# A new hand-listed order of the same steps for chunked attention and a gated convolution

## The chip, the cores and the metric

The kernel runs on one core of one Trainium2 chip. The metric is device microseconds of that core for one execution. A core has TensorE (the profile's PE, with PEld for its weight loads), VectorE (DVE), ScalarE (ACT), GpSimd (POOL) and SyncE (SP), each with an in-order queue of instructions of its own, and 16 DMA engines that move data between HBM and the on-chip memory. The profile is of one execution.

## The reference

Four sequences of 768 tokens go through attention with 8 heads of width 64, then through a gated causal convolution with two 512x512 products. Attention is chunked: each block of 32 queries sees 8 memory keys, 16 keys to the left, its own 32 and 8 to the right, 64 in all.

```python
for c in range(nc):                                   # 24 chunks of 32
    k_full = concatenate([mem_k, k[:, :, l_start:r_end]], axis=2)
    v_full = concatenate([mem_v, v[:, :, l_start:r_end]], axis=2)
    scores = scale * matmul(q_c, k_full.transpose(0, 1, 3, 2))
    a = exp(scores - max(scores)); a = a / (sum(a) + 1e-09)
    out[:, :, c_start:c_end] = matmul(a, v_full)
# x: (4, 768, 512), the heads side by side
gate_pre = sum over k of conv_w[k] * xp[:, k:k + S, :]     # 5 taps, causal
return (sigmoid(gate_pre) * (x @ w_val)) @ w_out
```

The inputs of attention are float32; w_val, w_out and conv_w come as float64 (in bits) and are turned into float32 on the chip.

## The kernel before

**Steps and their order.** The kernel is written as 1269 named steps, each a few instructions, and a string ORDER (line 69) that lists them all as engine:name, with T for TensorE, V for VectorE, A for ScalarE, G for GpSimd and S for SyncE, the latter three also issuing DMAs. `Plan.run` (line 45) walks through the string and calls each step's function for the engine that is named there, so the string fixes both the order of every engine's queue and, for steps that have two or three ways, the engine. The framework adds a semaphore wait wherever an instruction needs something that another engine has yet to do. It counts two accesses of one PSUM tile by different engines as such a case even where both only read; the one that is later in the string waits for the other.

**Buffers.** The numbers of buffers are in CAPS (line 22): one PSUM bank for all transposes of q, k and the probabilities (`t=1`), one pair of banks for scores and for the values' product (`a=1`), two banks for transposed x (`x=2`), three for the FFN accumulators (`f=3`), two buffers each for loaded k, q and weights.

**Units.** The attention is cut into 20 units, each a pair of heads with 256, 512 or 768 tokens: units 0 to 3 have the first 256 tokens of the first sequence, 4 to 7 its other 512, and 8 to 19 the other sequences whole. For unit u the steps are: `lk`, `lq`, `lv` (loads; `zv` and `zm` clear value tiles first, `mv` fills the memory values and `mk` the memory keys into their tiles); `tk`, `tq` (TensorE transposes, line 569) with their copies out of PSUM `ek`, `eq`; `sc` (scores, line 639); `mx`, `ss` (maximum and shift, VectorE, lines 660 and 664); `ex` (ScalarE, line 672); `tp` and `ep` (probabilities transposed and copied); `va` (values, line 690); `nd`, `ni`, `nx` (normalising, lines 706 to 713). Then `tx` transposes the result into an x tile in PSUM (line 750, one or two tiles a unit, 36 in all). The x tile has up to nine readers: `xh` (its rounded high part, ScalarE or VectorE), `xl` (the rest, VectorE, after xh), `cv` five times (the taps of the convolution; the first, `cv.._4`, on ScalarE at line 802 or VectorE at 804, the other four on VectorE at 798), and `hs`, `hp` (four columns that pass between the parts of a sequence). `ga` is the gate's tanh (ScalarE, line 822).

**FFN pieces.** Tokens go through the two products in eight pieces of 256, 512 and six times 384 columns: `f1_n_<co><ci>` (three products of high and low parts, line 848), `h` (gate times value, line 854), `hh`, `hl` (its high and low part), `f2_n_<g><ci>` (three products, line 903), `oe` (copy out, lines 933 and 934) and `st` (store, line 944). The last output tile is done in two halves; the second half's steps end in `_`.

**Weights.** `lw0` to `lw7` load 512 KB each; `wv01` to `wv08` (and `wo..`) turn one 128-row slice of them from float64 into float32, steps 1, 2, 3, 6 and 7 on VectorE (lines 355 to 382), 4 and 5 on ScalarE, 8 on GpSimd or VectorE (line 388); `wv0h` and `wv0` split it into a high and a low part. `lcw` and `cw1` to `cw8` do the same for the convolution weights. Lines 246, 249, 252 and 264 are helpers: copy on ScalarE, VectorE and GpSimd, and a subtraction.

The part of ORDER around unit 4's x tiles, in the string before:

```
S:lw6 V:wo17 T:va5
A:cv4_1_4 T:f1_0_31 T:tx4_0 A:mv7 V:cv4_1_0 V:nd5 A:xh4_0 T:tq7_0 V:cv4_1_1 V:ni5 V:cv4_1_2 A:xh4_1
V:xl4_1 T:f1_0_32 T:f1_0_33 A:eq7_0
```

Of the kernel before, what the change touches and what calls it, by code (L numbers as in the profile page):

```python
# [80 lines left out]
V:cv0_0 V:nx2 A:hs1 V:cv1_0 S:lk5 A:eq5_0 S:lk6 T:tp3_0 A:ep3_0 V:wv33 T:tx2_0 V:wv37 A:ga1 A:xh1_0
A:xh2_0 G:wv2 T:va3 T:tq4_0 S:lv4_1 T:f1_0_10 V:wo01 V:cv2_0_4 A:wv35 G:wv38 A:wo04 A:eq4_0 V:wo02
T:f1_0_00 V:nd3 V:wo03 V:ni3 T:tk5_0 V:xl1_0 A:wo05 A:ga0 S:lq6 G:mv5 A:ek5_0 V:nx3 S:lw5 A:wv3h
V:wo06 V:xl2_0 T:sc4 V:cv2_0_0 V:cv2_0_1 V:wo07 V:mx4 S:lv5_1 V:hs2 T:tx3_0 T:f1_0_11 V:ss4
A:cv3_0_4 S:lv4_0 T:tk6_0 T:sc5 A:ex4 V:cv3_0_0 A:ek6_0 T:tp4_0 T:f1_0_12 A:ep4_0 V:cv3_0_1 G:wv3
V:wo11 T:f1_0_01 V:mx5 V:wo12 V:ss5 A:wo14 A:xh3_0 V:cv2_0_2 T:tq6_0 V:wo13 A:eq6_0 V:cv2_0 A:ex5
# [6 lines left out]
T:tx5_0 T:sc7 A:ex6 A:xh5_0 S:lv6_1 V:cv4_0_2 A:ga2 V:xl5_0 V:cv4_0 A:eq8_1 V:mx7 T:tp6_0 A:wo1h
A:ga4 A:hp5 V:wo27 S:lv6_0 T:tx5_1 A:ep6_0 G:hl0_0 T:tk8_1 V:ss7 T:f1_0_23 S:lw7 V:h0_3 V:wo23 G:wo1
V:h0_2 A:cv5_0_4 V:cv5_0_0 V:cv5_0_1 T:f2_0_00 T:va6 A:cv5_1_4 A:ex7 V:cv5_1_0 V:nd6 T:f2_0_01
V:cv5_0_2 V:ni6 S:lv7_1 A:hh0_3 A:wo25 A:ek8_1 T:tp7_0 A:hh0_2 V:wo31 V:cv5_1_1 V:nx6 A:ep7_0 S:lq9
V:cv5_0 T:f2_0_10 T:f1_1_00 A:mv9 T:tk8_0 A:xh5_1 T:tx6_0 G:mv8 V:wo32 V:cv5_1_2 S:lk9 V:xl5_1
A:ek8_0 V:cv5_1 A:wo34 A:xh6_0 G:hl0_2 G:wo28 V:hp6 V:wo33 T:va7 G:hl0_3 T:tx6_1 A:cv6_0_4 A:wo2h
V:wo36 T:tq9_0 T:f2_0_11 S:lq10 A:mk9 T:f1_1_01 A:eq9_0 V:wo37 G:wo2 A:cv6_1_4 A:wo35 V:nd7 V:xl6_0
T:tk9_0 T:f2_0_12 A:ek9_0 A:mk8 T:tk9_1 V:cv6_0_0 V:ni7 V:nx7 T:f2_0_02 G:wo38 V:cv6_1_0 A:xh6_1  # L100
A:ek9_1 V:cv6_0_1 V:cv6_1_1 A:wo3h V:xl6_1 G:wo3 T:tq9_1 A:eq9_1 T:sc8 V:cv6_1_2 V:cv6_0_2 V:cv6_1
V:cv6_0 T:tq10_0 T:f1_1_02 T:tx7_0 V:mx8 V:ss8 S:lv8_0 S:lk11 A:eq10_0 T:tx7_1 T:tq10_1 V:cv7_1_4
T:f2_0_03 A:xh7_0 A:eq10_1 V:xl7_0 G:mv10 V:hp7 T:sc9 A:ex8 A:oe0_0 T:tp8_0 V:xh7_1 A:cv7_0_4
V:cv7_1_0 S:lv8_1 V:xl7_1 S:lk10 A:ep8_0 T:f1_1_03 T:tp8_1 V:mx9 V:ss9 V:cv7_0_0 A:ep8_1 T:f2_0_13
T:f1_1_10 T:tk11_1 V:cv7_0_1 A:ex9 V:h1_0 T:va8 S:lv9_1 A:oe0_1 A:ga5 V:ek11_1 T:f1_1_11 V:cv7_0_2
T:tp9_0 V:nd8 A:ep9_0 V:cv7_0 T:f1_1_20 S:lv9_0 S:lq11 V:ni8 V:nx8 T:f1_1_12 V:cv7_1_1 V:cv7_1_2
T:tp9_1 V:mk11 A:mv11 T:tx8_0 T:f1_1_30 V:cv7_1 A:ep9_1 T:f1_1_21 T:tk10_1 V:cv8_0_4 V:cv8_0_0
T:f1_1_13 V:xh8_0 A:ga6 V:xl8_0 T:tx8_1 V:h1_1 A:ek10_1 T:tk10_0 A:cv8_1_4 V:cv8_1_0 S:lq12 T:va9
V:cv8_0_1 V:nd9 S:lv10_1 A:ek10_0 S:lv10_0 T:tk11_0 A:hh1_1 T:f1_1_22 A:hh1_0 A:xh8_1 A:ek11_0
# [869 lines left out]
```

## Time and profile before

| | |
|---|---|
| three runs | 270.07, 266.08, 269.98 us; median 269.98 |
| profiled execution, first to last instruction | 269.1 us |
| around it, against the runs at 269.98 and 270.07 | about 0.9 us |
| TensorE busy | 238.3 us (89%) |
| VectorE busy | 218.2 us (81%) |
| ScalarE busy | 127.9 us (48%) |
| GpSimd busy | 80.0 us (30%) |
| data moved | 34.96 MB, mean 130 GB/s |

Busy time is the time in which at least one instruction of the engine runs. A row of a timeline has the start, the length, the engine, the line, the operation and the tiles it writes and reads; in square brackets stands how long the engine was idle just before and what ended that. TensorE's clock is given as the share that was granted, 1.00 being 2.4 GHz.

### The profile page before, as it was taken

The page shows a single profiled execution, that of the slowest core. Times are in us where ns is not written, and L with a number is a line of the kernel's source. Part 1 is how long each engine was busy: PE and PEld are TensorE (multiplying, and loading weights), DVE is VectorE, ACT ScalarE, POOL GpSimd, SP SyncE. Part 2 cuts the span into 40 slices and gives each one's busy share as a digit, 9 for nine tenths or more (in the row PEclk, how much of TensorE's full clock was granted, in tenths as well). Part 3 has the DMA queues.
Part 4 walks back from the last instruction along what each step waited for, and adds up shares of the span by engine and source line. Part 5 has one row for each costly group of instructions (what it writes and reads, how often), then busy time and mean ns, then how long its engine had stood idle before and what let it go on. Part 6 is the DMA issues. An engine that isn't in the chain of part 4 may idle for free.

```text
span 269.1 us, 9694 instructions
## 1 busy us (share of the span) xinstructions
PE 238.3 (89%) x4158; PEld 200.2 (74%) x4158; DVE 218.2 (81%) x462; ACT 127.9 (48%) x259; POOL 80.0 (30%) x93
## 2 busy tenths in 40 slices
...
GB/s 151 177 198 207 211 178 183 117 210 180 177 137 147 144 186 178 44 132 137 165 164 132 160 149 55 106 163 187 101 143 2 4 168 44 80 0 39 78 48 111
DMA packets 99601, 34.96 MB, mean 130 GB/s; under 512 B 96082, under 2 KB 96358, under 8 KB 99558
## 3 DMA queue, kind: packets, MB, share of 16 engines
...
HBM read 28.03 MB, written 6.29 MB: 128 GB/s over the span
## 4 chain that ended last, share of the span: by engine, by line
PE 76%; DVE 12%; ACT 3%; issue 3%; DMA 3%; SPq 1%; POOL 1%; ACTq 0%; DVEq 0%
PE op L903 25%; PE vp L848 24%; PE sp L639 6%; PE xps L690 6%; PE tpx L750 4%; PE tq L569 4%; PE tk L569 4%; PE tp L569 4%; DVE gate L798 2%; DMA qn<-in_q_dram 2%; DVE e_wo L382 1%; DVE xn L713 1%; DVE e_wo L355 1%; SPq L493 1%; DMA craw<-in_moe_conv_w_dram 1%
## 5 line engine op out<-in xcount | busy, mean ns | idle before, releaser
L798 DVE SCALAR_TENSOR_TENSOR gate<-tpx,cw,gate 128x384 f32<-128x384 f32 (+9 forms) x144 | 79.3, 563 | 1.3 <-ACT gate L802 0.2
L264 POOL TENSOR_TENSOR hl<-h,hh 128x384 fp32r<-128x384 f32 (+2 forms) x25 | 26.0, 1044 | 107.6 <-DVE hh L249 55.2
L848 PE MATMUL vp<-xh,wv_hi 128*128 128x384 f32 (+2 forms) x128 | 49.1, 384 | 0.0
L848 PE MATMUL vp<-xl,wv_hi 128*128 128x384 f32 (+2 forms) x128 | 43.9, 343 | 0.0
L848 PE MATMUL vp<-xh,wv_lo 128*128 128x384 f32 (+2 forms) x128 | 43.9, 343 | 0.0
L903 PE MATMUL op<-wo_hi,hh 128*128 128x512 f32 (+1 forms) x100 | 41.9, 419 | 0.0
L903 PE MATMUL op<-wo_lo,hh 128*128 128x512 f32 (+1 forms) x100 | 38.6, 386 | 0.2 <-POOL wo_lo L264 0.2
L903 PE MATMUL op<-wo_hi,hl 128*128 128x512 f32 (+1 forms) x100 | 38.5, 385 | 0.0
L639 PE MATMUL sp<-kT,qT 64*32 64x64 f32 x1536 | 21.7, 239 | 8.7 <-DVE ss L664 3.9
L639 PEld LDWEIGHTS sp<-kT,qT 64*32 64x32 f32 x1536 | 17.6, 113 | 15.0 <-issue 8.4
L848 PEld LDWEIGHTS vp<-xh,wv_hi 128*128 128x128 f32 x128 | 25.0, 195 | 2.0
L854 DVE SCALAR_TENSOR_TENSOR h<-gate,vp 128x384 f32<-128x384 f32 (+2 forms) x32 | 17.2, 548 | 10.9 <-PE vp L848 9.4
L848 PEld LDWEIGHTS vp<-xh,wv_lo 128*128 128x128 f32 x128 | 25.1, 196 | 0.9
L848 PEld LDWEIGHTS vp<-xl,wv_hi 128*128 128x128 f32 x128 | 24.8, 194 | 0.9 <-DVE xl L264 0.2
L690 PE MATMUL xps<-v,pT 64*32 64x65 f32 x1536 | 21.1, 233 | 4.3 <-ACT pT L246 2.5
L690 PEld LDWEIGHTS xps<-v,pT 64*32 64x32 f32 x1536 | 17.3, 109 | 9.8 <-issue 6.1
L246 ACT COPY pT<-tp 128x384 f32<-128x384 f32 (+2 forms) x27 | 12.9, 479 | 23.5 <-PE tp L569 23.3
L569 PE MATMUL tk<-ident,kn 128*128 128x128 f32 x96 | 18.2, 304 | 6.2 <-ACT memT L246 2.6
L802 ACT ACTIVATE gate<-tpx,cw 128x384 f32<-128x384 f32 (+1 forms) x27 | 14.6, 549 | 15.1 <-PE tpx L750 10.0
L903 PEld LDWEIGHTS op<-wo_hi,hl 128*128 128x128 f32 x100 | 18.8, 188 | 4.0
L252 POOL COPY v<-mv 104x1536 f32<-104x1536 f32 (+2 forms) x12 | 17.4, 1458 | 11.5 <-issue 9.9
L569 PE MATMUL tq<-ident,qn 128*128 128x128 f32 x96 | 18.8, 311 | 2.1 <-DMA qn<-in_q_dram 0.9
...
## 6 DMA issues: line engine op xcount, KB each, us to landing
...
```

What stands on the lines that cost most here:

```text
L246: return lambda: nc.scalar.copy(out(), in_())
L252: return lambda: nc.gpsimd.tensor_copy(out(), in_())
L264: return lambda: eng.tensor_tensor(out=out(), in0=a(), in1=b(), op=ALU.subtract)
L569: nc.tensor.transpose(U[name, i][:, (g - g0) * P : (g - g0 + 1) * P], src(g), ident)
L639: nc.tensor.matmul(U["sp"][CH * jc : CH * (jc + 1), j, g * WIN : (g + 1) * WIN], U["qT"][j * D : (j + 1) * D, g * P + CH * jc : g * P + CH ...
L690: nc.tensor.matmul(U["xps"][CH * jc : CH * (jc + 1), j, g * VW : (g + 1) * VW], U["pT"][j * D : (j + 1) * D, g * P + CH * jc : g * P + CH ...
L750: nc.tensor.transpose(U["x", i][:, o : o + P], U["xn"][:, g].rearrange("p j d -> p (j d)"), ident,)
L798: nc.vector.scalar_tensor_tensor(out=o, in0=i_, scalar=w, in1=o, op0=ALU.mult, op1=ALU.add)
L802: nc.scalar.activation(o, i_, AF.Copy, scale=w)
L848: nc.tensor.matmul(vp, w, x, start=ci == 0 and m == 0, stop=ci == NCT - 1 and m == 2)
L854: nc.vector.scalar_tensor_tensor(out=T["h", n, co][:, 0:nt], in0=bt[b, co]["gate"][:, t0 : t0 + nt], scalar=1.0, in1=T["vp", n, co][:, 0:n ...
L903: nc.tensor.matmul(op, x, w[:, ci, c0:c1], start=ci == 0 and m == 0, stop=ci == NCT - 1 and m == 2)
```

## The change

The string ORDER is replaced by another one with the same 1269 names; nothing else differs. 120 of the steps that can run on more than one engine are on another engine than before, and all five queues have another order. VectorE has 412 steps and no longer 429, ScalarE 278 (260), GpSimd 73 (78), SyncE 104 (100), TensorE 402 as before. The new string was made with the waits between ScalarE and VectorE on one PSUM tile counted. Of the 36 x tiles' readers the engine changes 56 times in the new string's order, where it changed 72 times.

The diff has 110 lines on each side; here are the beginning, the lines around unit 4's x tiles, and the end.

```diff
-G:ident V:bias0 S:mem A:bias S:lcw T:tmem A:lk0 V:cw1 A:cw4 A:emem01 S:lq1 A:emem00 V:emem11
-A:emem10 V:cw6 G:zk T:tk0_0 V:cw2 S:lq0 V:cw3 A:cw5 S:lw0 S:lw1 A:ek0_0 V:cw7 G:zv1 T:tq0_0 A:lk1
-V:eq0_0 G:zv2 V:wv01 V:mk0 T:tq1_0 S:lv1_1 V:mk1 A:wv04 A:eq1_0 V:wv02 V:wv11 G:cw8 T:sc0 V:mx0
-V:ss0 V:wv06 T:tcw G:zv0 A:cw A:wv14 G:zm A:ex0 S:lv1_0 V:wv03 S:lv0_0 T:tk1_0 A:ek1_0 V:wv12 V:wv07
-T:sc1 V:wv16 S:lv0_1 A:wv05 V:mx1 T:tp0_0 V:ss1 S:lk2 V:wv17 G:lw2 G:wv08 A:ep0_0 S:lq2 A:ex1 T:va0
...
-V:wv22 A:wv1h V:mv4 V:cv0_0_4 T:tq3_0 A:eq3_0 G:mv3 V:wv23 T:sc2 V:mx2 A:wv24 V:wv26 T:tx1_0 V:ss2
...
-A:cv4_1_4 T:f1_0_31 T:tx4_0 A:mv7 V:cv4_1_0 V:nd5 A:xh4_0 T:tq7_0 V:cv4_1_1 V:ni5 V:cv4_1_2 A:xh4_1
-V:xl4_1 T:f1_0_32 T:f1_0_33 A:eq7_0 G:wo0 A:wo15 A:hp4 T:tk7_0 V:nx5 V:wo21 V:xl4_0 T:sc6 A:cv4_0_4
...
-T:f2_7_22_ T:f2_7_20 T:f2_7_23_ T:f2_7_01 T:f2_7_21 T:f2_7_02 T:f2_7_22 S:st6_2 G:st6_1 S:st7_1
-A:oe7_2_ T:f2_7_03 A:oe7_0 T:f2_7_23 A:oe7_2 S:st7_2_ S:st7_0 S:st7_2
+S:mem G:ident A:lk0 T:tmem S:lcw G:zv1 S:lw0 S:lq0 V:zv0 V:bias0 V:zm G:zv2 A:emem10 A:bias V:emem01
+V:emem11 V:cw1 S:lq1 V:cw2 V:cw3 A:emem00 A:mk0 G:zk A:cw4 A:mk1 T:tk0_0 A:ek0_0 V:cw6 S:lv0_1
+V:wv01 A:cw5 V:wv02 A:wv04 V:cw7 V:wv03 T:tq0_0 V:wv06 A:eq0_0 S:lk1 S:lmv S:lv0_0 S:lv1_0 T:tq1_0
+A:eq1_0 G:lw1 T:sc0 V:cw8 T:tcw A:wv05 V:wv07 V:mx0 G:lw2 V:wv11 V:wv12 V:wv08 V:ss0 S:lk2 A:cw
...
+G:wv18 V:nx0 T:tx0_0 V:wv26 A:ek2_0 V:wv23 V:mv3 S:lq2 A:cv0_0_4 T:va1 S:lk3 V:nd1 V:ni1 A:xh0_0
...
+V:hs0 V:wo01 S:lq5 S:lq4 S:lv3_1 A:ek4_0 S:lv3_0 A:wv34 T:tp2_0 A:ep2_0 T:va2 G:mv5 A:ex3 A:xh1_0
+A:mv4 V:wv32 A:wo04 V:cv0_0 V:nd2 V:xl1_0 V:ni2 V:nx2 T:f1_0_00 T:tq5_0 T:tx2_0 T:f1_0_10 A:eq5_0
+T:tp3_0 V:wv36 A:cv2_0_4 V:wv33 T:f1_0_30 A:hs2 A:hs1 V:wv37 V:wo02 A:ep3_0 T:f1_0_11 S:lv4_1 A:wv35
...
+A:mv6 S:lv6_0 V:wo12 T:f1_0_33 A:ga1 V:nx4 A:wo24 T:tp5_0 T:f1_0_22 V:h0_1 T:tx4_1 A:ep5_0 S:lk8
+T:tx4_0 A:cv4_1_4 A:xh4_1 V:wo13 A:hp4 S:lv6_1 V:wo22 A:wo15 A:hh0_0 T:va5 V:wo17 A:cv4_0_4
+T:f1_0_23 V:cv4_1_0 T:tq7_0 A:eq7_0 G:hl0_0 V:nd5 G:wo18 V:cv4_1_1 A:xh4_0 V:ni5 A:hh0_1 S:lw7
...
+T:f2_7_01 S:st7_2_ T:f2_7_13 A:oe7_1 S:st7_1 T:f2_7_22 T:f2_7_02 T:f2_7_23 G:st6_1 T:f2_7_03 V:oe7_2
+S:st7_2 A:oe7_0 S:st7_0
```

Copies out of the transposes' bank that change engine: to ScalarE go ek2_0, ek11_1, ek15_0, ek15_1, ek17_1, ek18_1, eq0_0, eq13_1, eq16_1, eq19_0, eq19_1, ep16_0, ep17_0, ep17_1, ep19_0 and ep19_1; to VectorE ek12_0, ek18_0 and ep13_0.

## Rows read from the trace of the kernel before

**Rows 1.** Busy time by stage: stretch, length, each engine's busy us, clock, DMA share.
```profile
3.24:42.37 39.13, 23.38 (x384) 15.49 (x383) 35.57 (x81) 20.19 (x48) 20.63 (x20) 1.00 0.92 193
42.37:76.55 34.18, 28.86 (x578) 23.53 (x578) 32.22 (x76) 25.12 (x56) 14.01 (x13) 0.90 0.99 167
76.55:100.00 23.45, 23.45 (x583) 19.38 (x583) 22.59 (x50) 14.16 (x27) 5.85 (x5) 1.00 1.04 164
...
106.00:262.00 156.00, 155.05 (x2487) 135.65 (x2486) 124.78 (x251) 62.77 (x118) 34.01 (x38) 1.00 0.52 100
```

**Rows 2.** Timeline of TensorE: products behind its stops (idle time in brackets).
```profile
42.52 1.17 PE L639 MATMUL sp<-kT,qT 64*32 64x64 f32 x64 [2.63 <-DVE ss L664]
53.93 0.55 PE L569 MATMUL tk<-ident,kn 128*128 128x128 f32 x3 [1.54 <-ACT qT L246]
62.08 0.55 PE L569 MATMUL tk<-ident,kn 128*128 128x128 f32 x3 [0.65 <-ACT pT L246]
65.98 0.32 PE L690 MATMUL xps<-v,pT 64*32 64x65 f32 x9 [1.58 <-issue]
...
104.08 0.66 PE L639 MATMUL sp<-kT,qT 64*32 64x64 f32 x42 [2.11 <-issue]
```

**Rows 3.** Timeline of VectorE and ScalarE around unit 4's second x tile.
```profile
52.50 0.48 DVE L798 SCALAR_TENSOR_TENSOR gate<-tpx,cw,gate 128x256 f32<-128x256 f32 x1
53.02 0.37 ACT L246 CAST xh<-tpx 128x256 fp32r<-128x256 f32 x1 [1.36 <-DVE gate L798]
53.42 0.42 DVE L264 TENSOR_TENSOR xl<-tpx,xh 128x256 fp32r<-128x256 f32 x1 [0.44 <-ACT xh L246]
```

**Rows 4.** Timeline of VectorE, the first 24 us.
```profile
3.24 1.33 DVE L355 TENSOR_SCALAR e_cw<-craw 20x128 uint32<-20x128 uint32 x1 [2.34 <-DMA craw<-in_moe_conv_w_dram]
5.47 0.23 DVE L249 COPY memT<-tp_mem 64x64 f32<-64x64 f32 x1 [0.90 <-ACT memT L246]
...
8.20 0.42 DVE L249 COPY qT<-tq 128x256 f32<-128x256 f32 x1 [1.60 <-PE tq L569]
...
8.97 1.28 DVE L249 COPY kT<-memT 128x192 f32<-128x192 f32 x2
...
21.04 2.97 DVE L249 COPY v<-mv 104x1024 f32<-104x1024 f32 x1
```

**Rows 5.** Line 382 by itself: durations ns min/median/max, first and last start.
```profile
L382 DVE SCALAR_TENSOR_TENSOR e_wv<-raw_wv,e_wv x4: 677/682/1625, 13.2 to 33.4; 128x512 uint32<-128x512 uint32 x4
```

**Rows 6.** Timeline of GpSimd, the first 21 us.
```profile
6.98 0.45 POOL L388 TENSOR_TENSOR m_cw<-m_cw,e_cw 20x128 f32<-20x128 f32 x1 [2.28 <-ACT m_cw L374]
7.37 1.39 POOL L285 MEMSET v<- 128x1560 f32 x1
...
8.87 1.11 POOL L305 MEMSET mv<- 128x1024 f32 x1
...
14.97 1.28 POOL L388 TENSOR_TENSOR m_wv<-m_wv,e_wv 128x512 f32<-128x512 f32 x1
...
20.77 0.82 POOL L252 COPY v<-mv 104x512 f32<-104x512 f32 x1 [0.60 <-DMA mv<-in_mem_v_dram]
```

**Rows 7.** Groups by form: busy us, mean ns, idle before.
```profile
L246 ACT COPY pT<-tp 128x384 f32<-128x384 f32 x19 | 9.1, 478 | 16.4 <-PE tp L569 16.2
...
L264 DVE TENSOR_TENSOR hl<-h,hh 128x384 fp32r<-128x384 f32 x7 | 4.5, 641 | 1.2 <-ACT hh L246 1.2
...
L249 DVE COPY kT<-tk 128x384 f32<-128x384 f32 x6 | 3.3, 557 | 2.0 <-PE tk L569 2.0
```

**Rows 8.** Timeline of TensorE: 128x256 products before and behind the stop of 2.63.
```profile
39.16 0.28 PE L848 MATMUL vp<-xh,wv_lo 128*128 128x256 f32 x1
39.29 0.28 PE L848 MATMUL vp<-xl,wv_hi 128*128 128x256 f32 x1
...
44.75 0.41 PE L848 MATMUL vp<-xh,wv_lo 128*128 128x256 f32 x1
```

**Rows 9.** Timeline of ScalarE at the end: the last two copies of the output.
```profile
265.14 0.87 ACT L933 ACTIVATE o<-op 128x512 f32<-128x512 f32 x2 [2.46 <-PE op L903]
```

More of the change, by code (lines that the diff above doesn't have):

```diff
@@ L81 @@
[L81 to L86, printed above, removed]
@@ L93 @@
[L93 to L98, printed above, removed]
@@ L99 @@
[L99 to L109, printed above, removed]
-S:lk12 T:f1_1_31 G:hl1_1 V:cv8_0_2 V:ni9 T:tq11_0 A:ga7 T:f1_1_32 V:nx9 V:cv8_0 T:sc10 G:st0_0
@@ new lines @@
+S:lk17 A:ep13_1 T:f1_3_10 S:lq16 T:f1_3_33 T:f1_3_11 T:f1_3_20 V:cv12_1_0 V:h3_3 A:hh3_3 V:cv12_1_1
+V:hh2_3 T:f1_3_12 T:va13 V:nd13 V:ni13 G:hl2_3 T:tk14_1 G:hl3_3 T:f1_3_13 T:f2_2_10 A:ek14_1
+T:tq15_0 S:lv15_0 V:cv12_1_2 T:f1_3_21 A:xh12_0 A:xh12_1 A:eq15_0 T:f2_2_11 T:tk14_0 V:h3_1 V:nx13
+V:xl12_0 V:xl12_1 V:cv12_0_2 V:cv12_0 A:ek14_0 T:f1_3_22 T:f2_2_00 T:sc14 T:tx13_0 A:xh13_0 A:hh3_1
+T:tq16_0 V:cv12_1 V:mx14 V:ss14 G:mv16 A:eq16_0 V:cv13_0_4 V:cv13_0_0 V:cv13_0_1 A:mk18 A:ex14
+G:hl3_1 T:f2_2_01 S:lv15_1 T:tx13_1 T:f1_3_23 T:f2_2_02 T:tq15_1 A:eq15_1 A:xh13_1 T:f2_2_03
@@ new lines @@
+S:lv16_0 V:cv13_1_4 T:f2_2_12 V:cv13_1_0 A:oe2_0 V:h3_2 V:xl13_0 T:sc15 V:mx15 V:ss15 V:mk19
+T:tq16_1 V:cv13_1_1 V:cv13_1_2 V:cv13_1 A:eq16_1 T:f2_2_13 A:oe2_1 S:lk16 T:f2_2_20 T:tp14_0
+A:ep14_0 T:f2_2_21 T:f2_3_10 T:tp14_1 A:ep14_1 V:xl13_1 T:f2_2_22 T:f2_3_00 T:f2_2_23 A:oe2_2 T:va14
+G:mv17 S:st2_1 A:mk16 V:cv13_0_2 T:tk16_0 V:cv13_0 V:nd14 V:ni14 A:ex15 T:f2_3_11 V:nx14 A:ek16_0
+S:lv16_1 A:hh3_2 T:f2_3_20 T:tp15_0 A:ep15_0 A:ga12 T:tx14_0 V:xh14_0 V:hl3_2 A:cv14_0_4 V:cv14_0_0
+T:f2_3_21 V:xl14_0 V:cv14_0_1 V:cv14_0_2 T:tx14_1 A:cv14_1_4 G:st2_0 T:tp15_1 S:lq17 A:ep15_1
```

161 lines of the change are left out of this document (85 added, 76 removed).

## The prediction

> **What bounds the kernel now.** I read the engines' shares of the span first; they only say that TensorE and VectorE are both busy most of the time. Then the busy time by stage [rows 1]: from 3.24 to 42.37 us VectorE is busy for 35.57 of 39.13 us and TensorE for 23.38; from 42.37 to 76.55 VectorE has 32.22 and TensorE 28.86 of 34.18; from 76.55 to 100 both are full (22.59 and 23.45 of 23.45). From 106 to 262 TensorE is busy for 155.05 of 156 us, and VectorE has room. So there are two regimes: up to about 100 us VectorE sets the pace (it decodes the float64 weights beside the first attention units), and after it TensorE does, with 0.95 us idle in 156. An order of the same steps can gain in two ways: TensorE's long full stretch begins earlier, or the few stops ahead of it and in it go. Those stops are single rows of TensorE's timeline [rows 2]: 2.63 us before the scores of unit 5 (waiting for VectorE's shift of unit 4), 1.54 us at 53.93, 0.65 us at 62.08, and two of 1.58 and 2.11 us that no semaphore explains ("issue").
>
> The wait that the change counts can be seen once, whole [rows 3]. On the x tile of unit 4's second half ScalarE's copy xh comes between VectorE's taps and VectorE's xl. ScalarE sits idle for 1.36 us until the tap that starts at 52.50 has ended, although both only read that tile; VectorE then idles 0.44 us for xl; and the query copy behind xh in ScalarE's queue is late, which is the 1.54 us of TensorE at 53.93 [rows 2]. In the new order ScalarE does its tap and the xh of that tile back to back, ahead of VectorE.
>
> **Part 1: turns between ScalarE and VectorE.** I counted, for the 36 x tiles, how often their readers change engine in queue order: 72 times before, 56 after. The kind of turn that made the stop above, back from VectorE to ScalarE, falls from 12 to 4 in units 0 to 7 and stays at 10 in units 8 to 19. So what is removed lies in the first 100 us. There it is worth the 1.54 us on TensorE and the 0.44 us on VectorE. The other turns have no stop of TensorE beside them and are put at nothing, hidden by VectorE's other queued work; at most they give a second stop of that size.
>
> **Part 2: VectorE's load up to the shift of unit 8**, which lies near the end of its full stretch. I compared the two lists of VectorE's steps ahead of it. Gone are the first query copy (0.42), two fills of memory keys (1.28 together) and the fill mv4 of a value tile (2.97) [rows 4], one key copy (0.56) [rows 7] and two taps (0.48 each, as in rows 3): 6.2 us. All go to ScalarE, which is busy for 20.19 of 39.13 us there [rows 1]. Added after 3.24 us are a memory-key copy (0.23, as the one at 5.47 [rows 4]), the last step of the convolution weights (0.45 on GpSimd [rows 6]), the product wv08 and the fill mv3. wv08 takes 1.28 us on GpSimd (at 14.97 [rows 6]); VectorE's two-input subtraction of 384 columns takes 0.641 [rows 7], so 512 are 0.85 by its rate; ends 0.64 and 1.28, and I take 0.85. mv3 is half of mv4, so 1.5 us by VectorE's row of 2.97, or 0.82 by GpSimd's row of mv3 itself [rows 6]; I take 1.5, VectorE's own. That is 3.0 us. Two memsets, zv0 and zm, also come to VectorE (1.39 and 1.11 us on GpSimd [rows 6]), but ahead of 3.24 us, where VectorE sits idle for 2.34 us until the convolution weights have landed [rows 4]; they fit but for some 0.2 us, which I leave out (ends -0.5 and +0.5). Net: 3.2 us less.
>
> VectorE also loses 0.90 and 1.60 us early, waiting for ScalarE's memory-key copies and for the first query transposes [rows 4]. The query copy is no longer its own, and the first weight's load now stands ahead of the query loads in SP's queue, so that decode steps can fill that time. Ends 0 and 2.5; I take 1.1, a little under half, as the first scores still have to be waited for later in its list. With the 0.44 of part 1, VectorE is at the shift of unit 8 some 3.2 + 1.1 + 0.4 = 4.7 us earlier.
>
> One thing is left at nothing: the same step of the weight decoding takes 0.68 us on VectorE or 1.6 us [rows 5], the latter where a GpSimd step runs at the same time. GpSimd loses some 5 us of early work by the rows above, so fewer should meet; but where the rest falls can't be told from the lists: 0, with ends of -2 and +2 (two such steps).
>
> **Part 3: can TensorE follow?** Its list ahead of the scores of unit 5 gains six groups of the first FFN product (three 128x256 products each) and loses none. At 0.13 us a product (39.16 to 39.29 [rows 8]) that is 2.3 us of work put into a stretch where TensorE waits for 2.63 us. With the 1.54 us gone it is 3.8 us. Behind the stop of 2.63 us the same product takes 0.41 us instead of 0.28 [rows 8], and the granted clock is 0.90 in that stage [rows 1]: a fifth of it, 6.8 us, at 1.2 instead of 2.4 GHz, which costs 3.4 us. If a third of that goes, TensorE has 3.8 + 1.1 = 4.9 us in hand, as much as VectorE gives. Ahead of the scores of unit 8 the two lists of TensorE differ by one small transpose step, and behind them it is full; so what is gained by then reaches the end whole. I take 4.7.
>
> The Trainium skill, "TensorE: Matmul & The Clock Gate" (What's actually happening), says that the halved clock is the default and that sustained activity releases it. By that rule the denser start would give back more than my third, up to all of the 3.4 us; VectorE's pace would still hold TensorE, and the sum would stay.
>
> **Part 4: what it adds.** Sixteen PSUM copies (keys, queries, probabilities) go from VectorE to ScalarE and three come back; 14 and 3 of them lie after 100 us, 11 net, at 0.48 us each [rows 7]: 5.3 us more on an engine that is busy for 62.77 of 156 us there [rows 1]. Behind each of them in ScalarE's queue stand xh and the tanh, for which FFN products wait, and all transposes share one PSUM bank, so a late copy stops the next transpose: 0.65 us at 62.08 [rows 2]. After 106 us the old order has no such stop, since products stand between; I take two, 1.3 us; ends 0 and 11 x 0.65 = 7.2. One weight load goes from SP's queue to GpSimd's and one the other way, and the loads of k, q and v move with their units; the buffers that they wait for come free at the same steps as before, so 0. At the end the last output tile is one of 512 columns and no longer a half of 256: the two old copies take 0.87 us together [rows 9], the new one starts behind the last product alone; the larger store behind it is put at 0.1, ends -0.3 and +0.3.
>
> **Sum.** -4.7 + 1.3 + 0.1 = -3.3 us on a span of 269.1. Around the span lie some 0.9 us (two of the three runs are at 269.98 and 270.07, the first being the median): 270.0 - 3.3 = 266.7 us. The third run, 266.08, shows that runs of one kernel spread by as much as this gain.
>
> **Rivals.** *More goes than I count* (0.28). VectorE fills all of its 2.5 us of early waits, and TensorE's two unexplained stops, 1.58 and 2.11 us, go as the loads move: -3.3 - 1.4 - 3.7 = -8.4, so 261.6. For it: no step of the list needs these stops. Against it: the loads are the same bytes, and DMA is full in these stages in rows 1.
> *It removes what does not matter* (0.18). VectorE's pace early is set by its load and by the slow steps beside GpSimd. Two more slow ones (1.9) and unfilled early waits (1.1) leave 4.7 - 3.0 = 1.7 us, less the 1.4 added: -0.3, so 269.7.
> *ScalarE becomes the late one* (0.14), slower than before. Each of the 11 further copies stops TensorE for the 0.65 us of the row: -4.7 + 7.2 + 0.1 = +2.6, so 272.6. It decides from about eight such stops on. For it: TensorE has no slack after 106 us. Against it: ScalarE is at 40% there, and FFN products lie between the transposes.
>
> **How the numbers follow.** The forecast has 0.40, the rivals 0.28, 0.18 and 0.14. Two per cent, about what a measurement of this kernel can tell from no change, is 5.4 us: faster means under 264.6. The first rival lies beyond that, with some of the forecast's own spread: 0.34. Slower means over 275.4, which only the tail of the last rival reaches: 0.09. The rest is 0.57. The range goes from 259.5 (the first rival with the -2 of the GpSimd neighbours) to 273.0 (just past the last rival); the forecast alone would have 264 to 269.
>
> **What would show it.** Right: the scores of unit 5 start near 38 us instead of 42.52; TensorE's idle time ahead of 76 us is some us less, with no stop at unit 4's copies; from 100 us on TensorE is full again, some 4 us further in its list. Wrong: stops of TensorE behind ScalarE's copies after 106 us; more idle time of VectorE from 3.24 to 76.55 us than the old 5.5 us of rows 1; or scores of unit 5 no earlier than before.

## The result and the profile after

| | before | after |
|---|---|---|
| runs beside each other | 266.08 to 270.07 us, median 268.31 (4) | 256.9 to 261.0 us, median 258.18 (4) |
| ratio, 95% interval | | 0.963 [0.954, 0.971] |
| span of the profiled execution | 269.1 us | 259.2 us |
| TensorE / VectorE busy | 238.3 / 218.2 us | 235.9 / 204.9 us |
| ScalarE / GpSimd busy | 127.9 / 80.0 us | 134.9 / 73.8 us |

Faster by 10 us; the forecast was 3.3 us and the range ended at 259.5. The profiled execution after the change was the longest of its four, 261.0 us.

The busy time by stage, cut at the scores of units 5 and 8 as in [rows 1], and from 80 us on:

```profile
3.24:38.48 35.24, 24.73 (x403) 17.40 (x403) 29.68 (x81) 22.57 (x55) 14.48 (x22) 1.00 0.92 201
38.48:68.36 29.88, 25.98 (x557) 20.50 (x557) 26.56 (x69) 24.02 (x54) 13.00 (x14) 0.89 1.06 177
3.24:76.55 73.31, 57.76 (x1177) 43.60 (x1178) 63.34 (x168) 52.05 (x120) 31.10 (x40) 0.95 1.00 185
80.00:180.00 100.00, 100.00 (x1990) 86.89 (x1970) 85.50 (x170) 55.66 (x110) 25.18 (x23) 1.00 0.99 158
```

VectorE was busy for 35.57 us of the first stage and 32.22 of the second; now it is for 29.68 and 26.56. The scores of unit 5 start 4.04 us earlier and those of unit 8 8.19 us earlier. VectorE now idles for 9.97 us between 3.24 and 76.55 us, and from 80 to 180 us TensorE has no gap at all.

TensorE's stops after, in its timeline, answering to [rows 2]:

```profile
38.48 0.84 PE L639 MATMUL sp<-kT,qT 64*32 64x64 f32 x63
41.31 0.31 PE L639 MATMUL sp<-kT,qT 64*32 64x64 f32 x1 [2.00 <-issue]
54.40 0.55 PE L569 MATMUL tq<-ident,qn 128*128 128x128 f32 x3 [0.37 <-ACT qT L246]
55.68 0.86 PE L639 MATMUL sp<-kT,qT 64*32 64x64 f32 x64 [0.73 <-DVE ss L664]
...
75.03 1.01 PE L639 MATMUL sp<-kT,qT 64*32 64x64 f32 x78 [1.14 <-issue]
...
181.89 0.78 PE L690 MATMUL xps<-v,pT 64*32 64x65 f32 x56 [0.57 <-issue]
```

The stops behind VectorE and ScalarE shrank (2.63, 1.54, 0.65 before). Those that nothing explains did not go: 2.00, 1.14 and 0.57 us in other places.

**Where the 9.9 us of the two spans lie.** I cut both executions at VectorE's maximum over the scores of unit 3 and of unit 8; between these cuts TensorE does nearly the same work. First before, then after:

```profile
0.00:28.60 28.60, 14.66 (x227) 8.58 (x227) 22.10 (x51) 13.79 (x32) 15.25 (x30) 1.00 0.76 177
28.60:78.30 49.70, 39.59 (x835) 32.24 (x836) 47.43 (x112) 33.54 (x77) 23.65 (x21) 0.93 1.04 179
78.30:269.10 190.80, 184.04 (x3098) 159.36 (x3096) 148.70 (x300) 80.60 (x152) 41.06 (x44) 1.00 0.59 110
```

```profile
0.00:26.80 26.80, 14.07 (x227) 8.31 (x227) 21.04 (x56) 15.46 (x36) 12.98 (x26) 1.00 0.85 194
26.80:71.20 44.40, 39.54 (x839) 31.91 (x839) 39.75 (x105) 34.67 (x79) 19.91 (x21) 0.92 1.04 177
71.20:259.20 188.00, 182.29 (x3096) 158.54 (x3094) 144.10 (x286) 84.77 (x165) 40.90 (x41) 1.00 0.68 117
```

1.8 us come before the first cut, 5.3 between the cuts, 2.8 behind. In the middle TensorE is busy for 39.6 us both times: 5.3 us of its idle time went while VectorE's busy time fell from 47.43 to 39.75, that is by 7.7 us. This is the stretch to explain.

TensorE's waits of 0.15 us and more in it, by what ended them (total, times, longest us), first before, then after:

```profile
PE sp L639 <- DVE ss L664: 2.6, 1, 2.6
PE xps L690 <- issue: 1.6, 1, 1.6
PE tk L569 <- ACT qT L246: 1.5, 1, 1.5
PE xps L690 <- ACT pT L246: 1.4, 1, 1.4
PE tp L569 <- ACT qT L246: 1.1, 2, 0.7
...
```

```profile
PE sp L639 <- issue: 2.0, 1, 2.0
PE xps L690 <- DMA v<-in_mem_v_dram: 0.7, 1, 0.7
PE sp L639 <- DVE ss L664: 0.7, 1, 0.7
...
```

In all, waits that ScalarE ended fall from 4.6 to 0.6 us, and those that VectorE ended from 3.1 to 1.3. So the larger part stands directly behind ScalarE's copies. ScalarE's lateness hangs at least in part on VectorE: with ScalarE's queue as before, more work on VectorE raises both sums (7.3 and 6.9 us in vload_b below), and less work lowers both (3.4 and 2.5 in nosign). The new order of ScalarE's whole queue was not tried alone.

**VectorE's slow steps.** The decode line of [rows 5] after the change:

```profile
L382 DVE SCALAR_TENSOR_TENSOR e_wv<-raw_wv,e_wv x4: 673/683/686, 8.9 to 30.7; 128x512 uint32<-128x512 uint32 x4
L382 DVE SCALAR_TENSOR_TENSOR e_wo<-raw_wo,e_wo x4: 679/681/683, 35.6 to 67.0; 128x512 uint32<-128x512 uint32 x4
```

On this line no step of 1.6 us is left; the four e_wo steps were at 693/1548/1635 before. What made them slow is seen when GpSimd's and VectorE's timelines of the kernel before are laid side by side:

```profile
35.03 1.29 POOL L388 TENSOR_TENSOR m_wv<-m_wv,e_wv 128x512 f32<-128x512 f32 x1 [2.08 <-ACT m_wv L374]
35.22 1.65 DVE L366 SCALAR_TENSOR_TENSOR m_wo<-raw_wo,m_wo 128x512 f32<-128x512 uint32 x1
...
49.72 1.28 POOL L264 TENSOR_TENSOR wo_lo<-m_wo,wo_hi 128x512 fp32r<-128x512 f32 x1 [6.82 <-ACT wo_hi L246]
49.91 1.64 DVE L382 SCALAR_TENSOR_TENSOR e_wo<-raw_wo,e_wo 128x512 uint32<-128x512 uint32 x1
...
66.88 1.29 POOL L388 TENSOR_TENSOR m_wo<-m_wo,e_wo 128x512 f32<-128x512 f32 x1
66.95 1.50 DVE L355 TENSOR_SCALAR e_wo<-raw_wo 128x512 uint32<-128x512 uint32 x1
```

Each of these slow steps ends a fixed time behind the GpSimd step that was running when it came up: 36.87 - 36.32 = 0.55, 51.55 - 51.00 = 0.55, 68.45 - 68.17 = 0.28 us. So it waits for the whole GpSimd step and then takes most of its own 0.68 or 0.42 us. Only steps whose operands all lie in SBUF do so here. Steps that read PSUM keep their length: this tap, wholly beside a GpSimd step, takes 0.47 us, as taps do elsewhere (0.48 in [rows 3]).

```profile
68.12 0.93 POOL L264 TENSOR_TENSOR hl<-h,hh 128x256 fp32r<-128x256 f32 x1
68.37 0.47 DVE L798 SCALAR_TENSOR_TENSOR gate<-tpx,cw,gate 128x256 f32<-128x256 f32 x1
```

The Trainium skill, "SBUF — State Buffer" (Who interferes with whom), says that VectorE and GpSimd share a pair of SBUF ports and that "Whoever issues first gets the shared pair for the whole instruction; the other fully blocks", for some VectorE steps with one SBUF input, and that a step with two contends with a GpSimd step that reads SBUF; these rows agree.

The free length of a step is what it takes with no GpSimd step beside it: 0.42 or 0.69 us for the 128x512 steps and 0.22 for the first convolution step. Two rows of [rows 4] were slow as well. The value fill of 2.97 us and the two memory-key copies of 1.28 take this in turns and in from27, two of the runs below:

```profile
21.22 0.68 DVE L249 COPY v<-mv 104x1024 f32<-104x1024 f32 x1
...
10.02 0.41 DVE L249 COPY kT<-memT 128x192 f32<-128x192 f32 x2
```

Counting each step's time over its free length, the slow time ahead of unit 8 was 10.8 us in eleven steps, 5.7 of it before 27 us and 5.0 behind. After the change it is 1.8 us, 1.1 and 0.7. So of the 7.7 us in the middle stretch 4.3 are slow steps. Most of the other 3.4 did not go to another engine: by the two strings five steps, some 2.3 us (four taps and wv31), now stand ahead of unit 3's maximum, and only some 0.6 us net went to ScalarE (cv2_0_4, hs2 and hp6, with hs0 coming back). The slow time is not fixed by the order alone: turns, gates2 and late_new begin with the same steps as the kernel before, and have some 4.5 us of it before 27 us.

### The profile page after: what moved, and what is told of

It is laid out like the page before. It is cut to its first block, busy times and chain, and to the rows that moved or that the text cites. A ratio compares the mean times of both kernels' runs of the same rounds, so it can differ in the third digit from the quotient of the medians.

```text
span 259.2 us, 9693 instructions
## 1 busy us (share of the span) xinstructions
PE 235.9 (91%) x4158; PEld 198.8 (77%) x4158; DVE 204.9 (79%) x446; ACT 134.9 (52%) x278; POOL 73.8 (28%) x87
## 4 chain that ended last, share of the span: by engine, by line
PE 80%; DMA 9%; DVE 5%; ACT 3%; issue 2%; SPq 0%; ACTq 0%
PE vp L848 26%; PE op L903 24%; PE xps L690 7%; PE sp L639 6%; DMA v<-in_v_dram 5%; PE tpx L750 4%; PE tq L569 4%; PE tp L569 4%; PE tk L569 4%; DMA kn<-in_k_dram 2%; DMA v<-in_mem_v_dram 1%; DVE gate L798 1%; DMA mk_nat<-in_mem_k_dram 1%; ACT kT L246 1%; DVE xn L713 1%
## 5 line engine op out<-in xcount | busy, mean ns | idle before, releaser
L798 DVE SCALAR_TENSOR_TENSOR gate<-tpx,cw,gate 128x384 f32<-128x384 f32 (+8 forms) x144 | 78.8, 563 | 3.2 <-ACT xh L246 1.5
L264 POOL TENSOR_TENSOR hl<-h,hh 128x384 fp32r<-128x384 f32 (+2 forms) x25 | 25.2, 1012 | 85.8 <-ACT hh L246 60.9
L848 PE MATMUL vp<-xh,wv_hi 128*128 128x384 f32 (+2 forms) x128 | 48.5, 379 | 0.0
L246 ACT COPY pT<-tp 128x384 f32<-128x384 f32 (+2 forms) x31 | 14.9, 479 | 22.9 <-PE tp L569 22.5
L252 POOL COPY v<-mv 104x1536 f32<-104x1536 f32 (+1 forms) x12 | 16.8, 1404 | 32.2 <-PE xps L690 22.0
L246 ACT COPY kT<-tk 128x384 f32<-128x384 f32 x30 | 14.4, 481 | 20.5 <-PE tk L569 20.2
L639 PE MATMUL sp<-kT,qT 64*32 64x64 f32 x1536 | 20.7, 232 | 4.5 <-issue 3.1
L639 PEld LDWEIGHTS sp<-kT,qT 64*32 64x32 f32 x1536 | 16.9, 109 | 9.8 <-issue 7.7
L246 ACT COPY qT<-tq 128x384 f32<-128x384 f32 (+2 forms) x31 | 14.8, 478 | 15.6 <-PE tq L569 14.5
L246 ACT CAST hh<-h 128x384 fp32r<-128x384 f32 (+2 forms) x22 | 10.8, 499 | 21.5 <-DVE h L854 21.4
## 6 DMA issues: line engine op xcount, KB each, us to landing
qn<-in_q_dram SPq DMA_DIRECT2D x24, 192.0 KB
kn<-in_k_dram SPq DMA_DIRECT2D x24, 192.0 KB
v<-in_v_dram SPq DMA_DIRECT2D x24, 192.0 KB
```

Of the source, the lines that this page charges most:

```text
L246: return lambda: nc.scalar.copy(out(), in_())
L252: return lambda: nc.gpsimd.tensor_copy(out(), in_())
L264: return lambda: eng.tensor_tensor(out=out(), in0=a(), in1=b(), op=ALU.subtract)
L639: nc.tensor.matmul(U["sp"][CH * jc : CH * (jc + 1), j, g * WIN : (g + 1) * WIN], U["qT"][j * D : (j + 1) * D, g * P + CH * jc : g * P + CH ...
L798: nc.vector.scalar_tensor_tensor(out=o, in0=i_, scalar=w, in1=o, op0=ALU.mult, op1=ALU.add)
L848: nc.tensor.matmul(vp, w, x, start=ci == 0 and m == 0, stop=ci == NCT - 1 and m == 2)
```

## The experiments

All are compared with the kernel before on the same chip. "The stretch" is that from unit 3's to unit 8's maximum, in each run's own profile; "slow" is the slow time in it. Lines of strings show only the steps that the edit concerns, in their order.

| run | time, us | ratio to before | stretch | VectorE busy in it | slow |
|---|---|---|---|---|---|
| before | 268.3 to 270.0 | 1 | 49.7 | 47.4 | 5.0 |
| vload_b | 275.40 | 1.023 [1.017, 1.029] | 54.7 | 53.1 | 5.0 |
| vload_a | 263.29 | 0.979 [0.973, 0.984] | 48.0 | 47.4 | 2.7 |
| late_new | 268.94 | 0.995 [0.987, 1.003] | 51.1 | 47.1 | 4.7 |
| turns | 269.46 | 0.996 [0.988, 1.005] | 52.4 | 47.0 | 5.0 |
| prods | 268.51 | 1.003 [0.998, 1.007] | 48.0 | 46.4 | 4.2 |
| first27 | 270.11 | 1.005 [1.001, 1.010] | 50.6 | 45.4 | 4.3 |
| gates2 | 271.62 | 1.013 [1.008, 1.018] | 52.6 | 45.3 | 2.7 |
| split | 266.72 | 0.990 [0.986, 0.994] | 47.8 | 44.7 | 2.5 |
| gates | 269.42 | 0.996 [0.989, 1.004] | 47.4 | 44.6 | 2.3 |
| collide | 261.82 | 0.978 [0.971, 0.985] | 45.4 | 43.5 | 4.4 |
| nosign | 264.54 | 0.981 [0.974, 0.988] | 47.3 | 42.5 | 3.0 |
| pad_ctl | 260.73 | 0.977 [0.967, 0.988] | 45.0 | 41.4 | 2.1 |
| from27 | 262.50 | 0.977 [0.962, 0.992] | 45.1 | 40.9 | 0.0 |
| early_new | 263.00 | 0.972 [0.965, 0.980] | 43.5 | 40.0 | 0.7 |
| after | 258.18 | 0.963 [0.954, 0.971] | 44.4 | 39.8 | 0.7 |
| prods_back | 258.39 | 0.964 [0.953, 0.974] | 43.8 | 39.3 | 0.0 |
| nosign_a | 259.96 | 0.973 [0.963, 0.983] | 43.7 | 37.3 | 0.7 |

Down the last columns: with 44 us of VectorE and more, the stretch is VectorE's time and 0.5 to 3 us, unless another wait comes in (turns, first27 and gates2, each told below; late_new, with stops of TensorE of 2.95 us behind VectorE and 1.90 unexplained). With under 42 it stays at 43.5 to 45 us, however little VectorE has. At a threshold of 2% the change and early_new are faster, eng_only and ord_only slower; late_new, turns, prods, first27, gates, gates2 and split are the same, and the rest are unclear.

**Where in time: four hybrids.** Each takes one order up to a step and the other behind it; the lines show the joint.

```diff
 early_new: the new order up to V:ss8, the old behind
-T:f2_0_13 V:mx8 V:ss8 T:tq10_1 V:cv7_1_0
+T:f2_0_13 V:mx8 V:ss8 T:tq10_1 A:eq10_1 V:xl7_0 G:mv10
 late_new: the old up to V:ss8, the new behind
+T:tx7_0 V:mx8 V:ss8 G:mk11 S:lv8_1 S:lv8_0
 first27: the new up to V:ss3, the old behind
+T:sc3 V:mx3 V:ss3 S:lq5 V:mv4 A:ex2
 from27: the old up to V:ss3, the new behind
+V:mx3 V:cv1_0_1 V:ss3 G:wv28 V:wv31 V:cv1_0_2
```

> The new order up to the shift of unit 8, and from there on the order and the engines of before. If the gain comes from the first 80 us (theories A, B and C all say so): 7 to 10 us faster than before, near the changed kernel. If the later part has a share of its own: 3 to 6 us faster.

> The order of before up to the shift of unit 8, and from there on the new order and its engines. If the gain comes from the first 80 us: within 1.5 us of before, either way. If ScalarE's further copies cost something (the third rival): 1 to 3 us slower. If the later part has a share of the gain: 2 to 5 us faster.

> The changed kernel's order and engines up to the softmax subtraction of unit 3 (at 27.3 us in the changed kernel), and behind it the rest in the order and on the engines of before. If the gain of the stretch before 80 us comes from what left VectorE in the first 27 us (the early copies and clears of the prediction): 263.5 to 266 us. If it comes from the order behind that: 267 to 270 us.

> The reverse: the kernel before up to the softmax subtraction of unit 3, and behind it the rest in the order and on the engines of the changed kernel. If the gain comes from the first 27 us: 266 to 269 us. If it comes from the order behind: 259 to 262.5 us. If both halves hold on to each other, as order and engines did, neither half alone gives more than a third of the gain.

The part up to unit 8 alone gives three quarters of the gain; the part behind it alone 0.5%, at most 1.3%. The first 27 us alone give nothing: its profile reaches unit 3's maximum 2.0 us earlier, and has lost most of it by unit 4's (40.7 us against 41.0), with TensorE stopped for 1.7 us by a load of memory values; a stop of 3.0 us behind the softmax follows ahead of unit 5's scores. So what counts is mainly the new order from 27 to some 75 us, as far as hybrids show it: from27 has the new end as well, and its interval is wide.

**Order and engines.** The change does both. eng_only keeps the old order and moves the 120 steps, ord_only keeps the old engines:

```diff
 eng_only
-A:emem01 S:lw1 A:lk1 V:eq0_0 V:mk0 V:mk1 G:cw8 G:zv0
+V:emem01 G:lw1 S:lk1 A:eq0_0 A:mk0 A:mk1 V:cw8 V:zv0
...
 ord_only
-V:emem01 G:lw1 S:lk1 A:eq0_0 A:mk0 A:mk1 V:cw8 V:zv0
+A:emem01 S:lw1 A:lk1 V:eq0_0 V:mk0 V:mk1 G:cw8 G:zv0
...
```

> The order of the kernel before, word for word, with each step on the engine that the change gives it. Theory D (engines): VectorE's early load falls as in the prediction, 262 to 264.5 us. Theory A (collisions): the order still lets GpSimd run beside VectorE's decode steps; 265.5 to 269 us, with five or more decode steps at 1.1 us or longer before 77 us.

> The order of the changed kernel, with each step left on the engine that it has before the change. Theory A: most of the decode steps keep clear of GpSimd; 260 to 263 us. Theory D: with the old load on VectorE the kernel keeps under a third of the gain; 266 to 269 us.

Both expectations missed by far: 281.2 us, ratio 1.052 [1.044, 1.059], and 289.15 us, ratio 1.079 [1.069, 1.089]. A queue's order is made for the steps that stand in it; TensorE's waits in the two show it, eng_only first (total, times, longest us):

```profile
PE tpx L750 <- DVE gate L798: 6.0, 7, 1.5
PE xps L690 <- DVE ss L664: 4.6, 2, 3.6
```

```profile
PE sp L639 <- ACT kT L246: 7.6, 1, 7.6
PE tp L569 <- DVE qT L249: 4.5, 1, 4.5
```

So the gain can't be shared out between "engines" and "order"; only VectorE's sum can be priced.

**The counted waits alone.** In turns only ScalarE's readers of the x tiles of units 0 to 7 move together, as in:

```diff
-A:cv4_1_4 V:cv4_1_0 A:xh4_0 V:cv4_1_1 V:cv4_1_2 A:xh4_1 V:xl4_1
+A:cv4_1_4 A:xh4_1 V:cv4_1_0 A:xh4_0 V:cv4_1_1 V:cv4_1_2 V:xl4_1
```

> The order of before, with only ScalarE's readers of the x tiles of units 0 to 7 (xh, the first tap, the halo copies) moved up next to each other, so that no such tile goes back from VectorE to ScalarE (12 such turns before, 4 in the new order, 0 here); two halo copies change to ScalarE. Theory B: 4 us or more faster than before, with the stop of 1.54 us at unit 4's query copy gone and VectorE idle less. Theory A: 1 to 2 us faster, as the prediction's part 1 has it, and the slow decode steps beside GpSimd stay as many.

No gain. Its profile is of an execution of 274.41 us, where the median is 269.46, and holds an unexplained stop of 2.77 us and a granted clock of 0.75 from 60 to 70 us, so its stretch is longer than VectorE's time explains. The timed runs decide: taking this wait away alone is worth less than can be measured.

**TensorE's products.** prods brings five groups of products forward in TensorE's old queue, prods_back puts three back in the new one:

```diff
 prods
-T:f1_0_10 T:f1_0_00 T:tk5_0 T:sc4 T:tx3_0 T:f1_0_11 T:tk6_0 T:sc5
+T:f1_0_10 T:f1_0_00 T:f1_0_30 T:tk5_0 T:sc4 T:tx3_0 T:f1_0_11 T:f1_0_01 T:f1_0_31 T:tk6_0 T:sc5
 prods_back
-T:tk6_0 T:f1_0_32 T:sc5 T:tp4_0 T:f1_0_03 T:f1_0_13
+T:tk6_0 T:sc5 T:tp4_0 T:f1_0_03 T:f1_0_13 T:f1_0_30 T:f1_0_31 T:f1_0_32
```

> The kernel before with TensorE's queue alone changed: five groups of products of the first piece (f1_0 30, 01, 31, 02, 32; 0.97 us each by the rows of 128x256 products) stand earlier, as in the change, so that three accumulations are open instead of two, and three more groups lie ahead of the scores of unit 5, where TensorE stood idle for 2.63 us. Theory E (TensorE gains because it has products to do where it waited): 265 to 267 us against about 269, and the stop ahead of unit 5's scores falls below 1 us. Theory F (VectorE paces this stretch, and the products only move): no change, 268 to 270 us, the idle time comes back within the next two units.

> The changed kernel with three groups of products (f1_0 30, 31, 32) put back behind the others, as they stood before the change; 2.9 us of TensorE work leave the stretch ahead of unit 5's scores. Theory E: 2 to 3 us slower than the changed kernel, 260 to 262 us. Theory F: 257 to 259.5 us.

prods does not move the time, and leaves the stop ahead of unit 5's scores at 2.14 us: theory E falls. Both expectations put a group at 0.97 us, the sum of its rows' lengths, but these rows overlap; by their starts a group takes 0.36 us at the full clock (39.95 to 40.31 us in prods_back). So E's gain would have been 1 to 2 us. prods allows 0.5 us at most (0.998); prods_back, known to 1% either way, can't tell. Work that fills TensorE's stop ahead of unit 5 is missing a little later, as long as VectorE releases units at its own pace.

**The price of VectorE's time.** Ten idle steps more in either kernel, and the sign step of eight blocks left out of either:

```diff
 vload_b, vload_a
+    pad = const.tile([P, 512], F32, name="pad")
+            {"V": lambda: nc.vector.tensor_tensor(out=pad, in0=pad, in1=pad, op=ALU.mult)},
-V:wv32
+V:pv0 V:wv32
...
 nosign, nosign_a
+            if np_ < P:
-            nc.vector.scalar_tensor_tensor(
+                nc.vector.scalar_tensor_tensor(
```

> The kernel before with ten idle VectorE steps more (a 128x512 multiplication in SBUF, some 0.69 us each by the same step of the changed kernel), each ahead of a decode step between 27 and 75 us; nothing of the computation is left out. Theory V (VectorE paces this stretch before the change): 5 to 8 us slower than before, 274 to 277 us. Rival (waits from one engine to the next pace it, and VectorE's idle time takes the steps up): within 2 us of before.

> The same ten VectorE steps in the changed kernel. Theory V: VectorE has some 7 us of room between 20 and 80 us there, so under 4 us slower than the changed kernel, 258 to 262 us. Rival: the same cost as in the kernel before, whatever that is.

> The kernel before without the decode step that puts the sign bit into the exponent word, in the eight weight blocks of 128x512 (its weights lose their sign; the eight steps took 9.1 us of VectorE in the profile of before, four of them slow). Theory V: TensorE follows until its own work and the loads bound it, 261 to 264.5 us. Rival: 267 to 269 us.

> The changed kernel without the eight decode steps that put the sign bit in (its weights lose their sign; they take 5.4 us of VectorE in its profile, none of them slow). If VectorE still paces the early part after the change: 3 to 5 us off, 253.5 to 255.5 us. If TensorE, its loads and its own waits have become the bound: under 1.5 us off, 256.5 to 259 us.

The stretch of vload_b, nosign, vload_a and nosign_a, in this order:

```profile
27.70:82.40 54.70, 39.61 (x835) 31.71 (x836) 53.05 (x123) 33.77 (x77) 24.88 (x21) 1.00 0.96 170
```

```profile
27.30:74.60 47.30, 37.58 (x836) 29.74 (x836) 42.49 (x107) 33.61 (x76) 22.11 (x21) 1.00 1.08 185
```

```profile
25.50:73.50 48.00, 39.02 (x839) 30.70 (x839) 47.44 (x116) 35.08 (x78) 19.98 (x22) 0.96 1.08 175
```

```profile
26.50:70.20 43.70, 36.57 (x835) 29.37 (x834) 37.28 (x101) 33.16 (x76) 18.76 (x20) 1.00 1.08 181
```

In the kernel before, 5.6 us more of VectorE (53.05 against 47.43) lengthen the stretch by 5.0 us and the run by 2.3% (6 us). So added time costs about 0.9 us for 1 us: VectorE paces there. Time taken away gives less: in nosign 4.9 us less shorten the stretch by 2.4 us, with an unexplained stop of 2.68 us in it where before has 1.58, and the run by 1.9% (5 us); gates and split, below, give 0.7 to 0.8 us of the stretch for 1 us. In the changed kernel 7.7 us more cost 3.6 us of the stretch and some 4 to 5 us of the run, a little over what theory V allowed; 2.5 us less give 0.7 us of the stretch and nothing of the run (259.96 us, above both ranges expected). So the change took VectorE's time down to where something else holds the stretch at 43.5 to 45 us. TensorE is busy for 36.5 to 39.6 us of it; what the other 5 to 8 us wait for differs from run to run (4.3 us for loads in nosign_a, 4.5 for VectorE in from27), and no run settles it.

**The slow steps themselves.** collide brings slow steps into the changed kernel, pad_ctl is its control; gates, gates2 and split were to take them out of the kernel before.

```diff
 collide, pad_ctl
+        nc.gpsimd.tensor_copy(seen[i], flags[i])
+        nc.gpsimd.tensor_tensor(out=pad, in0=pad, in1=pad, op=ALU.mult)
+        step(f"fk{i}", {"V": lambda i=i: nc.vector.memset(flags[i], 1.0)})
+        step(f"gk{i}", {"G": lambda i=i: pad_step(i)}, after=[f"fk{i}", "pad"])
-V:ni0 V:wv13
+V:fk1 G:gk1 V:ni0 V:wv13
...
 gates
-V:wo03 V:ni3
+V:wo03 V:fk1 G:gk1 G:wv38 V:ni3
...
 gates2
-V:wo07 V:mx4
+V:wo07 V:fk1 G:gk1 G:wv3 V:mx4
...
 split
-            eng.tensor_tensor(out=R["mf"], in0=R["mf"], in1=R["ef"], op=ALU.mult)
+            for j in range(0, n, P if eng is nc.gpsimd else n):
...
```

> The changed kernel with nine idle GpSimd steps added (a 128x512 multiplication of a tile of its own by itself, some 1.3 us), each released by a one-column VectorE memset that stands one step ahead of a decode step of the experts' weights, so that the GpSimd step runs when VectorE comes to an SBUF-only step. Nothing of the computation is left out. Theory A (VectorE's SBUF-only steps wait for a GpSimd step that is already running, and this carries about half of what the change gave): VectorE's busy time before 80 us grows by 6 to 9 us, and the kernel takes 262 to 265 us against some 258 us for the changed kernel. Theory D (the work that left VectorE for other engines and the order of the products carry the gain): VectorE has room by then, and the kernel stays within 257 to 260.5 us.

> The control: the same nine idle GpSimd steps and nine VectorE memsets, but each released ahead of two or more VectorE steps that read PSUM, away from the decode steps. Nothing of the computation is left out. Both theories: 257 to 260.5 us, VectorE's busy time before 80 us within 2 us of the changed kernel's. If it is as slow as its partner, the added GpSimd work itself is what costs, and not its meeting with VectorE.

> The order of before, with six GpSimd steps of the weights held back (by a one-column copy that waits for a one-column VectorE memset) until the VectorE decode step that each met has run: wv18 behind wv21, wv38 behind wo03, wv3 behind wo07, wo0 behind wo17, wo1 behind wo27, wo28 behind wo31. Theory A (VectorE's SBUF-only steps stand still while a GpSimd step runs, and fewer such meetings are the part of the gain that was not forecast): the six steps fall from 1.0-1.65 us to 0.4-0.7, VectorE's busy time falls by about 5 us, and the kernel is 3 to 5 us faster than before. Theory B (turns between ScalarE and VectorE on the x tiles are the gain): VectorE is done earlier but waits for ScalarE instead; 0 to 1 us faster. Theory C (the moved steps are the gain): 1 to 2 us.

> The kernel before with seven GpSimd steps between 33 and 70 us (wv3 8, wv3, mv5, wo0 8, wo1 8, wo1, wo2 8) each held back, by a flag that VectorE sets, to the start of a stretch of VectorE steps that read PSUM; two VectorE, ScalarE and SyncE steps that wait for one of them move behind it. Nothing is left out. Before 27 us all stays as it was. If the slow steps fall from 6.7 us of extra time to under 3.5, theory V expects 3 to 4 us off at its price of 0.85 to 1 us per us, 265 to 267.5 us; the rival (slow steps are hidden anyway) expects 268 to 270.5. If the slow steps stay over 5 us, the run tells nothing.

> The kernel before with each GpSimd step of 128x512 in the decode and the low halves done as four of 128x128; nothing is left out. If a VectorE step waits only for the GpSimd instruction that is running, the slow steps fall from 6.7 us of extra time to under 3. Theory V then expects 264 to 267 us, and the rival 267.5 to 270. If VectorE's steps wait as long as before, or GpSimd's longer work makes its results late, this run tells nothing of the pace.

collide has nearly the slow time of the kernel before again (8.5 us ahead of unit 8, 4.4 in the stretch), and yet runs only 3.6 us over the changed kernel, between the ranges of both theories, and 1.1 us over its control (ratios 0.978 and 0.977, the same within their intervals). The control is not clean: it is just past its own range and has slow steps of its own, 2.1 us in the stretch. Once VectorE has room, slow steps are mostly covered. That alone would speak against theory A. The other side was harder to get. gates moved the six meetings, and five other steps became slow; in the stretch 2.7 us of slow time went and so did 2.3 us of its length, but the run is the same as before: its profile is 192.0 us long behind the stretch where before has 190.8, with unexplained stops of TensorE of 1.87 and 0.61 us (before: 2.11 and 0.47). gates2 brought the slow time in the stretch from 5.0 to 2.7 us, but the held-back fill mv5 stands ahead of a value load in SyncE's queue, and TensorE waited for that load:

```profile
50.23 1.29 PE L691 MATMUL xps<-v,pT 64*32 64x65 f32 x64 [4.14 <-DMA v<-in_v_dram]
```

It was my edit's fault and says nothing of the slow steps. split halved the slow time in the stretch too, and is the one of the three that keeps its gain: 1.0% [0.6, 1.4], 3 us for 2.7 us of VectorE. (The 6.7 us in two of the expectations count the decode steps alone, from the start to unit 8; by that count split still has some 4.8 us and gates2 5.7.) What stays open is the kernel before without its slow steps and with nothing else changed; no such order was found. That 4.3 us of the stretch are slow steps is therefore a count of rows; that VectorE's time there is what the length follows is what the runs show.

No version beats the changed kernel: prods_back, 258.39 us, is the same within its interval.

## Why the prediction was wrong, point by point

- *VectorE sets the pace up to about 100 us, TensorE follows and the rest moves with it.* Right in the main: vload_b prices added time on VectorE at about 0.9 us for 1 us, though time taken away gave 0.5 to 0.8 of the stretch, and the scores of unit 5 came at 38.48 us, as foretold (near 38). That this number fits is luck in part: ahead of them the slow time fell by 6.5 us (7.6 to 1.1), which the sum had at nothing.
- *Part 1, the counted wait.* It went: ScalarE's tap and xh of unit 4's second half now stand together (49.10 and 49.48 us), and the 1.54 us of TensorE became 0.37. But turns shows that it is worth nothing alone, so the 0.44 in the sum stood for nothing, and the words with which the change was made don't name what gave the time.
- *Part 2, 3.2 us of load.* Its rows of 2.97 and 1.28 us were themselves slow (0.68 and 0.41 free), and so is the new mv3 (1.50; 0.41 in collide). At free lengths the moved steps make some 2 us; the 3.2 held slow time without knowing it. VectorE's busy time up to unit 8's maximum fell from 69.5 to 60.8 us, with the two clears (2.3 us) left aside as in the prediction by 11.0: 9.0 of slow time and 2.0 of steps. 1.8 us came ahead of unit 3's maximum, where slow time fell too, so what the early waits (1.1) gave is not known; alone they are worth nothing (first27).
- *"One thing is left at nothing."* This is the step that failed. The slow steps were put at 0 with ends of 2 us either way, and were 4.3 us in the stretch and 9.0 up to unit 8. I had looked at one line's durations [rows 5] and saw a few slow steps; lines 366 and 355, the convolution weights' 1.33, the memory-key copies and the fill of 2.97 us [rows 4] hold the rest. The eleven slow rows with GpSimd's timeline beside them add up to 10.8 us. That sum, less the 3.2 that part 2 takes away with its two slow rows, was the lower end, not two steps; with it the first rival's 261.6 goes to 254.
- *Part 3, 4.9 us in hand.* Too low, and for other reasons: TensorE's idle time in the stretch alone fell by 5.3 us (10.1 to 4.9). The part counted two stops; waits of 1.4 and 1.1 us behind ScalarE's copies went too, and products in the place of a stop gain nothing by themselves (prods). The clock did not rise as I had it: 0.93 granted before and 0.92 after.
- *Part 4, two stops behind ScalarE, +1.3.* None is there: from 80 to 180 us TensorE is full, and behind 80 us no stop of 0.15 us or more is ended by ScalarE. late_new shows no cost either.
- *The rivals.* "More goes than I count" came nearest in time, for another reason: the unexplained stops add up to 3.7 us after, against 4.6 before. "It removes what does not matter" named the slow steps as what sets the pace, but let them grow by two. "ScalarE becomes the late one" is not seen.
- *What would show it.* The scores of unit 5 came as said; TensorE's idle time fell, though 0.37 us of a stop at unit 4's copies stayed; TensorE is full again, some 7 us further and not 4. The sign of failure in VectorE's idle time was chosen wrongly: it rose from 5.5 to 9.97 us because VectorE lost more work than TensorE could use.

The forecast had 3.3 us and the spans differ by 9.9. Of the 6.6 between, 2.4 lie ahead of unit 8's maximum (7.1 us earlier, where the sum had 4.7), 1.4 are part 4's costs, and 2.8 lie behind unit 8, where the prediction had no gain of its own.

The sum with the measured terms: the stretch gives 5.3 where VectorE's 7.7 us meet the next bound, 1.8 come ahead of it, 2.8 behind it (1.05 of TensorE's idle time, 1.75 of its busy time in nearly the same instructions); 9.9 in all. The busy time goes with the string: behind unit 8's maximum TensorE is busy for 182.1 to 183.2 us in the eight profiles that have the new string there, and for 183.6 to 185.9 in the ten that have the old (eng_only and ord_only left out); why is open. The idle time holds unexplained stops, 3.0 us before and 1.7 after, and how much of it is order is not settled: late_new's 0.995 [0.987, 1.003] allows anything from 0 to 3.5 us for the whole part behind unit 8.
